# When accumulating loads may start, and weights split two units at a time

## The chip, the cores and the metric

The kernel runs on one core of a Trainium2 chip. The metric is the time of one execution on the device in microseconds (us). The core has a matrix engine (TensorE, PE in the profile), a vector engine (VectorE, DVE), an engine for activation functions (ScalarE, ACT), a general one (GpSimd, POOL) and one that mainly issues transfers (SyncE, SP). Transfers run on 16 DMA engines that all queues share.

## The reference

Three steps follow each other, all in fp32:

- Attention on q, k, v of shape (4 batches, 8 heads, 576 positions, 64). Every position attends to its neighbours at a distance under 4 (the local part). Beside it, q, k and v are averaged over groups of 4 positions, a full softmax attention runs over the 144 averaged positions, and its output is repeated 4 times and added (the down-sampled part).
- The 2304 token rows of 512 go through a gated layer: `silu(x @ w_gate) * (x @ w_val) @ w_out`, inner width 1536.
- Then through a second layer: `h = x @ w_in`, `h * clip(h + 3, 0, 6) / 6 @ w_out`, inner width 2048.

## The kernel before

**Blocks and units.** The token rows are worked in five blocks of 8, 6, 8, 8 and 6 groups of 64 rows, so that matmuls have 512 or 384 columns. Each block runs 68 units. A unit is one slab of 128 inner columns of a weight: G, V and O for the first layer (36 units, phase 1), H and P for the second (32 units, phase 2). One unit is about 12 matmuls, which `run_unit` issues (L951 for G, V, H; L993 for O, P).

**Weights.** Each fp32 number is split into a high and a low part, and three products are summed. The split of a unit's weights is `split_unit`: a ScalarE copy of 128x512 writes the high part (L234), a VectorE subtraction of 128x512 writes the low part (L235). They go into the tile `wr`, which has four buffers of one unit. In block 0 the weights arrive as 64-bit numbers of 512 KB a unit (`load_raw`, tile `w`, four buffers); `decode_a` on ScalarE (L214) and `decode_b` on VectorE (L223) make fp32 of them, in pairs of units in a staging tile of three buffers, and ScalarE's queue stores each pair to memory (`kept`, L229). Blocks 1 to 4 load these pairs back on SP's queue (`load_kept`, L182, 512 KB a pair) into the same staging buffers. `prefetch(i)`, called at every unit, says how many units ahead each step runs: raw load 8, kept load 6, decode 5 and 4, split 2 (`LS`).

**The down-sampled part.** For batches 1 to 3, `down_sums` fills three tiles dnq, dnk and dnv with sums over four positions: GpSimd's queue issues 24 transfers of 144 KB per batch (L295), the first of each tile plain and the next three accumulating into it, so that the four of one half of one tile follow each other. The order is position by position, and q, k, v within one. The work for batch b+1 is interleaved with block b: at every odd unit of phase 1 one step is issued, first the transfers, then TensorE's transposes of q and k (L306, from unit 25 on); in phase 2 `down_main` runs scores, softmax and values (L876 to L909). The last reader of dnv is the matmul pO (L726). GpSimd has nothing else to do then, so its queue runs ahead of the program until a buffer isn't free.

**The local part.** Chunks of q, k and v are loaded on SP's queue by `load_chunk` (L130), and VectorE works scores (L785, L788) in phase 1 and values (L822 to L828) in phase 2; `step_x` transposes the result (L842) and adds the down-sampled part (L851) for a block two further on.

**Batch 0** is done in `first_batch` ahead of block 0, with a pool of its own: its tile `fvd` holds the sums of v, `fpT` (two buffers) the transposed probabilities. The transfers of `down_sums(1)` are issued in it.

**Order.** Instructions are placed on each engine by a planner that works with estimated costs; `keep_in_program_order` marks those that it may not move ahead of what stands before them. Each engine, and each queue, then runs its list in that order. `put_out` at a block's end copies the outputs to the tile `os` on ScalarE (L1018) and stores them.

Of the kernel before, what the change touches and what calls it, by code (L numbers as in the profile page):

```python
# [10 lines left out]
F32 = mybir.dt.float32  # L11
F32R = mybir.dt.float32r
BF16 = mybir.dt.bfloat16
I32 = mybir.dt.int32
I16 = mybir.dt.int16
I64 = mybir.dt.int64
F16 = mybir.dt.float16
AF = mybir.ActivationFunctionType
ALU = mybir.AluOpType
AX = mybir.AxisListType  # L20

P = 128
# [5 lines left out]
BLOCKS = [8, 6, 8, 8, 6]  # L28

CUTS = [[3, 2], [2, 2, 2, 2], [3, 2, 3], [3, 3], []]  # L30
LR, LD, LA, LB, LS = 8, 6, 5, 4, 2
WARM = 14
HALVES = 1
CLOAD = (0, 4)
# [11 lines left out]
def tile_kernel(  # L46
# [12 lines left out]
    nc = tc.nc  # L59

    B, H, S, D = q.shape
    DM = H * D
# [4 lines left out]
    NJH = NJ // 2  # L67
    W = 7
    NC = DM // P
# [7 lines left out]
    UMAX = max(BLOCKS)  # L77
# [6 lines left out]
    sp = ctx.enter_context(tc.tile_pool(name="sp", bufs=2))  # L84
# [3 lines left out]
    def bank(tag, name, bufs=1):  # L88
        return pp.tile([P, 512], F32, tag=tag, name=name, bufs=bufs)
# [10 lines left out]
    consts = cp.tile([P, SMALL // 4], F32, name="consts")  # L100
# [27 lines left out]
    def late(eng, dst, src):  # L128

        tc.keep_in_program_order(eng.dma_start(dst, src))  # L130
# [3 lines left out]
    def behind(ins):  # L134

        if front[0]:
            tc.keep_in_program_order(ins)
# [5 lines left out]
    units = []  # L143
# [17 lines left out]
    w32 = {}  # L161
    split = {}

    def view(t, i):
        return t[:, i % 2, :].rearrange("p (c e) -> p c e", c=NC)
# [63 lines left out]
            defer(1, lambda: nc.scalar.dma_start(kept[i // 2], t))  # L229

    def split_unit(i):
        s = view(w32[i // 2], i)
        r = sp.tile([P, 2, NC, P], F32R, tag="wr", name=f"wr{i}", bufs=4)
        behind(nc.scalar.activation(r[:, 0], s, AF.Copy))  # L234
        behind(nc.vector.tensor_tensor(r[:, 1], s, r[:, 0].bitcast(F32), op=ALU.subtract))  # L235
        split[i] = r

    def prefetch(i):
        steps = ((LR, load_raw), (LD, load_kept), (LA, decode_a), (LB, decode_b), (LS, split_unit))
        for ahead, fn in steps:  # L240
            if 0 <= i + ahead < len(units):
                fn(i + ahead)


    tick_no = [0]
# [24 lines left out]
        nc.vector.tensor_tensor(dst[:, :, 1], xv, dst[:, :, 0].bitcast(F32), op=ALU.subtract)  # L270


    nat = {}
    dn, qk = {}, {}

    def load_down(b, what, half, hh, alloc, eng):
        src = {"q": q, "k": k, "v": v}[what]
        t = alloc(f"n{what}{b}_{half}{hh}")
        late(
            eng, t,  # L280
            src[b, hh * 4:hh * 4 + 4, half * NJH * 4:(half + 1) * NJH * 4, :].rearrange("h (j t) d -> j h t d", t=4),
        )
        nat[b, what, half, hh] = t

    keys = [(w, half, hh) for w in "qkv" for half in range(2) for hh in range(2)]

    def down_sums(b, dn, qk, alloc, bufs, eng, lag=0):
        for w in "qkv":
            dn[w] = sp.tile([NJH, 2, H, D], F32, tag="dn" + w, name=f"dn{w}{b}", bufs=1)
        for t in range(4):  # L290
            for w in "qkv":
                src = {"q": q, "k": k, "v": v}[w]
                for half in range(2):
                    s_ = src[b, :, half * NJH * 4:(half + 1) * NJH * 4, :].rearrange("h (j t) d -> j t h d", t=4)[:, t]
                    tc.keep_in_program_order(nc.gpsimd.dma_start(  # L295
                        dn[w][:, half], s_, **({"accum_op": ALU.add} if t else {})))
                yield

    def sums_T(b):
        for w in "qk":  # L300
# [20 lines left out]
    def first_batch():  # L321

        QT = 122
        WK = QT + 6
        NT = -(-S // QT)
        GT = 6
        TT = S // GT
        with tc.tile_pool(name="fp", bufs=1) as fp:
# [36 lines left out]
            nc.gpsimd.memset(band[:, :, 2, nl - 3:nl], NEG)  # L365


            vd = fp.tile([NJH, 2, H, D], F32, name="fvd")

            def load_vd(n):  # L370
                hh, half = divmod(n, 2)
# [40 lines left out]
            load_vw(4)  # L412
            assert NT == 5
            prefetch(2 - LR)

            tmp = spare("tmp")
# [110 lines left out]
            def size(i):  # L527
                return min(QT, S - QT * i)
# [49 lines left out]
                )  # L578

            pT = {}  # L580

            def trans(i):
                n = size(i)
                w_ = n + 6
                pT[i] = fp.tile([WK, NC, 2, QT], F32, tag="fpT", name=f"fpT{i}", bufs=2)
                for hh in range(2):
                    ps = bank(f"acc{2 + hh}", f"fPT{i}_{hh}")[:, :4 * QT]
                    ps = ps.rearrange("p (c a s) -> p c a s", c=2, a=2)
                    for m in range(4):
                        nc.tensor.transpose(  # L590
                            ps[:w_, m // 2, m % 2, :n], pe[i][:n, 2 * hh + m // 2, m % 2, :w_], ident[:n, :n]
                        )
                    to = pT[i][:w_, 2 * hh:2 * hh + 2, :, :n]
                    nc.scalar.activation(to, ps[:w_, :, :, :n], AF.Copy)
# [39 lines left out]
                    put_cols(bi, t0 + a - starts[bi] * UT, xf[:, :, a:e])  # L634
                    a = e

            turns = [0]

            def spare_tile(name):

                turns[0] += 1
                if turns[0] % 3 == 0:
                    return fp.tile([NJH, H // 2, 4, D], F32, tag="vnat", name=name, bufs=2)
                t = fp.tile([TT, GT, H // 2, D], F32, tag="fnat", name=name, bufs=4)
                t = t.rearrange("j t h d -> j (t h d)")[:NJH, :2 * H * D]
                return t.rearrange("j (h t d) -> j h t d", h=H // 2, t=4)


            ahead = down_sums(1, dn, qk, spare_tile, 6, nc.sync)
            for c in range(NC):  # L650
                load_T("q", c)
                load_T("k", c)
# [146 lines left out]
    def chunk_exp(b, c, n):  # L799
        sc, _ = pes[b, c]  # L800

        tc.keep_in_program_order(nc.scalar.activation(sc, sc, AF.Exp, scale=0.125))
# [129 lines left out]
    state = {}  # L932
# [98 lines left out]
    b, u = 1, 0  # L1031
    for n in chain(*CUTS):
# [3 lines left out]
        if u == NG:  # L1036
            b, u = b + 1, 0
# [4 lines left out]
    def load_ahead(n):  # L1042
        nonlocal loaded
        while loaded < min(n, len(chunks)):
            load_chunk(*chunks[loaded])
            loaded += 1

    NAT = 4

    def nat_tile(name):  # L1050
        t = sp.tile([P, 4 * DM + 32], I16, tag="w64", name=name, bufs=NAT).bitcast(F32)
        return t[:NJH, :2 * H * D].rearrange("j (h t d) -> j h t d", h=H // 2, t=4)

    for bi in range(NB):
        mine = chunks[at:at + len(CUTS[bi])]
        at += len(mine)
        limit = starts[bi + 2] if bi + 2 <= NB else 0

        db = bi + 1 if bi + 1 < B else None

        def first_half():
            for m, ch in enumerate(mine):
                for _ in chunk_scores(*ch):
                    yield
                load_ahead(at - len(mine) + m + 3 if m + 3 <= len(mine) else loaded)
            for _ in range(VAL0.get(bi, 0)):
                unit_values()
                yield

        def weigh(ch):  # L1070
            chunk_exp(*ch)
            vq.extend((*ch, i) for i in range(ch[2]))

        def second_half():
            for ch in mine[1:] if bi in VAL0 else mine:
                weigh(ch)
            while vq:
                unit_values()
                yield

        gens = [first_half(), second_half()]
        sizes = [sum(CUTS[bi]) + VAL0.get(bi, 0), sum(CUTS[bi]) - VAL0.get(bi, 0)]
        main = iter(())
        sums = iter(())
        if db:
            sums = down_T(db, dn, qk)
            if bi:
                sums = chain(down_sums(db, dn, qk, nat_tile, NAT, nc.sync, lag=1), sums)
        for i in range(bi * NU, (bi + 1) * NU):
            m = i - bi * NU  # L1090
            prefetch(i)
            if m in CLOAD:
                load_ahead(at - len(mine) + min(CLOAD.index(m) + 1, len(mine)))
            if m == EXP_AT and bi in VAL0:
                weigh(mine[0])
            run_unit(i)
            ph = 0 if m < NU1 else 1
            if m == NU1:
                for _ in gens[0]:
                    pass  # L1100
                for _ in sums:
                    pass
                if db:
                    main = down_main(db, dn, qk)
            lo_, n_ = (0, NU1 - 2) if ph == 0 else (NU1, NU - NU1 - 6)
            mm_ = m - lo_
            for _ in range(sizes[ph] * (mm_ + 1) // n_ - sizes[ph] * mm_ // n_ if mm_ < n_ else 0):
                next(gens[ph], None)
            if m % 2:
                next(sums, None)  # L1110
            next(main, None)
            if m == NU - EARLY:
                load_ahead(at + 1)
            step_x(limit)
            next_tick()
        if bi + 1 < NB:
            for _ in gens[1]:
                pass
            for _ in main:
                next_tick()  # L1120
            while x_done[0] < starts[bi + 2]:
                step_x(limit)
                next_tick()
# [30 lines left out]
```

## Time and profile before

| | |
|---|---|
| median of 3 runs | 981.95 us (980.12 to 983.34) |
| the profiled execution's own time | 982.72 us |
| its span, first to last instruction | 980.9 us |
| busy: TensorE / VectorE / ScalarE / GpSimd | 944.0 / 748.5 / 528.5 / 106.8 us |
| mean granted TensorE clock | 0.979 of full speed |
| transfers on GpSimd's queue | 43488 packets, 10.72 MB, 10.9% of the 16 DMA engines' span |

Busy time is an average over stages that differ. A TensorE that is shown as busy is not always at its peak, since matmuls are pipelined and their ends are modelled. What a change is worth is read where TensorE's list has a gap.

### The profile page before, as it was taken

The page shows a single profiled execution, that of the slowest core. Times are in us where ns is not written, and L with a number is a line of the kernel's source. Part 1 is how long each engine was busy: PE and PEld are TensorE (multiplying, and loading weights), DVE is VectorE, ACT ScalarE, POOL GpSimd, SP SyncE. Part 2 cuts the span into 40 slices and gives each one's busy share as a digit, 9 for nine tenths or more (in the row PEclk, how much of TensorE's full clock was granted, in tenths as well). Part 3 has the DMA queues.
Part 4 walks back from the last instruction along what each step waited for, and adds up shares of the span by engine and source line. Part 5 has one row for each costly group of instructions (what it writes and reads, how often), then busy time and mean ns, then how long its engine had stood idle before and what let it go on. Part 6 is the DMA issues. An engine that isn't in the chain of part 4 may idle for free.

```text
span 980.9 us, 13441 instructions
## 1 busy us (share of the span) xinstructions
PE 944.0 (96%) x4800; PEld 795.3 (81%) x4800; DVE 748.5 (76%) x1237; ACT 528.5 (54%) x1115; POOL 106.8 (11%) x113
## 2 busy tenths in 40 slices
PE   8878999999799999999999999999999999999997
PEld 5666878777699987888888777788888788999996
DVE  6578976898789988999684699999346995555653
ACT  4685566985554557655333764453335445544653
POOL 5941000007300000460000000000000000000000
PEclk9788999999899999999999999999999999999999
DMA  8999899469985432596432213353322223533331
GB/s 210 183 277 323 291 332 301 151 227 233 297 248 185 161 126 66 137 241 211 159 120 86 80 51 108 141 203 110 105 91 103 86 93 113 161 129 124 122 127 48
DMA packets 116343, 160.82 MB, mean 164 GB/s; under 512 B 61868, under 2 KB 83756, under 8 KB 116276
## 3 DMA queue, kind: packets, MB, share of 16 engines
q1 hardware_dynamic: 67892, 131.41, 40.9%
q0 software_dynamic: 43488, 10.72, 10.9%
q10 hardware_dynamic: 4896, 17.83, 4.8%
q8 instruction: 38, 0.62, 0.3%
q14 instruction: 29, 0.24, 0.1%
HBM read 137.29 MB, written 22.54 MB: 163 GB/s over the span
## 4 chain that ended last, share of the span: by engine, by line
PE 66%; DVE 12%; DMA 5%; issue 2%; ACT 2%; SPq 0%; ACTq 0%; DVEq 0%
PE pH L951 15%; PE aP L993 14%; PE aO L993 12%; PE pV L951 11%; PE pG L951 10%; DVE wr L235 3%; DVE pv L822 2%; DMA w<-in_moe_w_out_dram 1%; DMA k<-in_k_dram 1%; DVE xf L851 1%; DMA w<-in_moe_w_in_dram 1%; PE pS L876 1%; DVE pv L826 1%; DVE gH L969 1%; DVE h L967 1%
## 5 line engine op out<-in xcount | busy, mean ns | idle before, releaser
L235 DVE TENSOR_TENSOR wr<-w,wr 128x512 fp32r<-128x512 f32 x340 | 231.9, 686 | 115.8 <-ACT wr L234 114.2
L234 ACT ACTIVATE wr<-w 128x512 fp32r<-128x512 f32 x340 | 212.4, 627 | 163.8 <-PE pV L951 53.8
L951 PE MATMUL pH<-x,wr 128*128 128x512 f32 (+1 forms) x960 | 213.6, 374 | 0.0
L993 PE MATMUL aP<-wr,gH 128*128 128x512 f32 x864 | 211.0, 394 | 0.1
L951 PEld LDWEIGHTS pH<-x,wr 128*128 128x128 f32 x960 | 174.2, 189 | 26.2 <-issue 3.1
L993 PEld LDWEIGHTS aP<-wr,gH 128*128 128x128 f32 x864 | 159.6, 188 | 34.1 <-issue 2.1
L951 PE MATMUL pG<-xr,wr 128*128 128x512 f32 (+3 forms) x732 | 160.1, 374 | 7.7 <-ACT xr L269 4.0
L951 PEld LDWEIGHTS pG<-xr,wr 128*128 128x128 f32 x732 | 135.8, 194 | 26.3 <-ACT xr L269 4.4
L951 PE MATMUL pV<-xr,wr 128*128 128x512 f32 (+1 forms) x720 | 153.6, 368 | 1.2 <-ACT sl L957 1.2
L993 PE MATMUL aO<-gV,wr 128*128 128x512 f32 (+1 forms) x720 | 154.3, 370 | 0.2 <-DVE wr L235 0.2
L993 PEld LDWEIGHTS aO<-gV,wr 128*128 128x128 f32 x720 | 132.3, 190 | 17.4 <-DVE wr L235 0.5
L951 PEld LDWEIGHTS pV<-xr,wr 128*128 128x128 f32 x720 | 130.8, 188 | 18.6 <-ACT sl L957 1.9
L966 ACT ACTIVATE h<-pH,consts 128x512 f32<-128x512 f32 (+1 forms) x80 | 51.4, 642 | 67.9 <-PE pH L951 67.8
L214 ACT ACTIVATE top<-w 128x512 f16<-128x512 bf16 x68 | 53.7, 792 | 40.2 <-DMA w<-in_moe_w_in_dram 10.3
L967 DVE SCALAR_TENSOR_TENSOR h<-h,pH 128x512 f32<-128x512 f32 (+1 forms) x80 | 50.4, 631 | 25.4 <-ACT h L966 24.8
L957 ACT ACTIVATE sl<-pG 128x512 f32<-128x512 f32 (+1 forms) x60 | 33.2, 553 | 64.6 <-PE pG L951 62.9
L785 DVE TENSOR_TENSOR pr<-q,k 128x1792 f32<-128x1792 f32 x27 | 54.5, 2018 | 9.2 <-DMA k<-in_k_dram 9.2
L295 POOL DMA_DIRECT2D dnv<-in_v_dram x24 | 38.3, 2021 | 190.1 <-PE pO L726 181.9
L969 DVE TENSOR_TENSOR gH<-h,gH 128x512 fp32r<-128x512 f32 (+1 forms) x80 | 50.6, 633 | 9.2 <-ACT gH L968 8.3
L822 DVE TENSOR_TENSOR pv<-sc,v 128x1792 f32<-128x1792 f32 x27 | 54.6, 2021 | 0.4
L788 DVE TENSOR_REDUCE sc<-pr 128x28 f32<-128x1792 f32 x27 | 54.3, 2011 | 0.1
L968 ACT ACTIVATE gH<-h 128x512 fp32r<-128x512 f32 (+1 forms) x80 | 46.9, 587 | 13.9 <-DVE h L967 11.9
(124 smaller groups left out, 767.3 us busy)
## 6 DMA issues: line engine op xcount, KB each, us to landing
w<-kept SPq DMA_DIRECT2D x136, 512.0 KB
kept<-w ACTq DMA_DIRECT2D x34, 512.0 KB
w<-in_moe_w_out_dram SPq DMA_DIRECT2D x28, 512.0 KB
w<-in_moe_w_in_dram SPq DMA_DIRECT2D x16, 512.0 KB
w<-in_moe_w_gate_dram SPq DMA_DIRECT2D x12, 512.0 KB
w<-in_moe_w_val_dram SPq DMA_DIRECT2D x12, 512.0 KB
out_dram<-os SPq DMA_DIRECT2D x16, 256.0 KB
dnq<-in_q_dram POOLq DMA_DIRECT2D x24, 144.0 KB, 9.7
```

The costliest lines, as they stand in the source:

```text
L214: behind(nc.scalar.activation(halves(top[i % 2], 2, F16)[:, :, 1], h3.bitcast(BF16), AF.Copy))
L234: behind(nc.scalar.activation(r[:, 0], s, AF.Copy))
L235: behind(nc.vector.tensor_tensor(r[:, 1], s, r[:, 0].bitcast(F32), op=ALU.subtract))
L785: nc.vector.tensor_tensor(pr, qt[:, a:a + SUB, None, :].to_broadcast([P, SUB, W, D]), win(kt, a, SUB), op=ALU.mult)
L788: nc.vector.tensor_reduce(sc[:, a:a + SUB], pr, axis=AX.X, op=ALU.add)
L822: nc.vector.tensor_tensor(pr, pe[:, a:a + SUB, :, None].to_broadcast([P, SUB, W, D]), win(vt, a, SUB), op=ALU.mult)
L951: nc.tensor.matmul(ps[:, cs], r[:, a, c], x[:, c, b_, cs], start=part is HIGH and a == c == 0, stop=part is LOW and c == NC - 1,)
L966: nc.scalar.activation(h, ps, AF.Relu, scale=1 / 6, bias=half1[:, 0:1])
L967: nc.vector.scalar_tensor_tensor(h, h, 1.0, ps, op0=ALU.min, op1=ALU.mult)
L968: nc.scalar.activation(g[:, 0, :nt], h, AF.Copy)
L969: nc.vector.tensor_tensor(g[:, 1, :nt], h, g[:, 0, :nt].bitcast(F32), op=ALU.subtract)
L993: nc.tensor.matmul(ps, **one, start=f_ == 0 and a == b_ == 0, stop=f_ == nf - 1 and b_ == 1,)
```

## The change

- `down_sums` for batches 2 and 3 begins with a GpSimd copy of one column out of `os` of the preceding block, taken from its third piece of outputs (e = 2). So all its transfers wait until that block's outputs are written.
- The order of its transfers is q and k first, all four positions, then v. The tiles are allocated at their first transfer.
- `split_unit` does nothing for odd units, and for an even one splits the pair with one ScalarE copy and one VectorE subtraction of 128x1024. `wr` has three buffers of a pair in the place of four of one unit. `LS` is 3, so units i+3 and i+4 are split at odd i; the pair of units 2 and 3 is split at unit 0.
- To make room, `fvd` takes the buffer of dnv, and `fpT` becomes two halves of one `wr` buffer.
- Functions that nothing called are gone.

```
-LR, LD, LA, LB, LS = 8, 6, 5, 4, 2
+LR, LD, LA, LB, LS = 8, 6, 5, 4, 3
...
     def split_unit(i):
-        s = view(w32[i // 2], i)
-        r = sp.tile([P, 2, NC, P], F32R, tag="wr", name=f"wr{i}", bufs=4)
-        behind(nc.scalar.activation(r[:, 0], s, AF.Copy))
-        behind(nc.vector.tensor_tensor(r[:, 1], s, r[:, 0].bitcast(F32), op=ALU.subtract))
-        split[i] = r
+        if i % 2:
+            return
+        s = w32[i // 2].rearrange("p u (c e) -> p u c e", c=NC)
+        r = sp.tile([P, 2, 2, NC, P], F32R, tag="wr", name=f"wr{i}", bufs=3)
+        behind(nc.scalar.activation(r[:, :, 0], s, AF.Copy))
+        behind(nc.vector.tensor_tensor(r[:, :, 1], s, r[:, :, 0].bitcast(F32), op=ALU.subtract))
+        split[i], split[i + 1] = r[:, 0], r[:, 1]
...
-            if 0 <= i + ahead < len(units):
+            if 0 <= i + ahead < len(units) and (fn is not split_unit or i != -1):
                 fn(i + ahead)
+        if i == 0:
+            split_unit(2)
...
+    def down_sums(b, dn, qk):
+        if b > 1:
+            done = state["os"]
+            tc.keep_in_program_order(nc.gpsimd.tensor_copy(consts[:, 60:61], done[:, (UMAX // 2 - 2) * DM:][:, :1]))
+        for ws in ("qk", "v"):
+            for t in range(4):
+                for w in ws:
+                    if t == 0:
+                        dn[w] = sp.tile([NJH, 2, H, D], F32, tag="dn" + w, name=f"dn{w}{b}", bufs=1)
+                    src = {"q": q, "k": k, "v": v}[w]
+                    for half in range(2):
+                        tok = src[b, :, half * NJH * 4:(half + 1) * NJH * 4, :].rearrange("h (j t) d -> j t h d", t=4)
+                        how = {"accum_op": ALU.add} if t else {}
+                        tc.keep_in_program_order(nc.gpsimd.dma_start(dn[w][:, half], tok[:, t], **how))
+                    yield
...
-            vd = fp.tile([NJH, 2, H, D], F32, name="fvd")
+            vd = sp.tile([NJH, 2, H, D], F32, tag="dnv", name="fvd", bufs=1)
...
+            turned = sp.tile([P, 2, 2, NC, P], F32R, tag="wr", name="turned", bufs=3).bitcast(F32)
+            turned = turned.rearrange("p u a c e -> p u (a c e)")
...
-                pT[i] = fp.tile([WK, NC, 2, QT], F32, tag="fpT", name=f"fpT{i}", bufs=2)
+                pT[i] = turned[:WK, i % 2, :NC * 2 * QT].rearrange("p (c a s) -> p c a s", c=NC, a=2)
```

## Rows read from the trace of the kernel before

**Rows 1.** Stretches: length; busy (count) PE, PEld, DVE, ACT, POOL; clock; DMA; GB/s

```profile
224.00:268.00 44.00, 37.26 (x163) 29.75 (x160) 34.60 (x63) 24.38 (x42) 26.73 (x20) 0.92 1.21 266
...
281.00:312.00 31.00, 31.00 (x181) 30.92 (x179) 24.84 (x32) 14.75 (x27) 0.00 (x0) 1.00 0.61 214
312.00:341.00 29.00, 28.80 (x171) 28.50 (x170) 28.97 (x44) 15.37 (x30) 0.52 (x1) 1.00 0.50 172
...
543.00:646.00 103.00, 102.46 (x501) 79.31 (x500) 93.94 (x177) 60.13 (x142) 0.00 (x0) 1.00 0.29 97
```

**Rows 2.** TensorE's instructions in order of time: start, us, line, what

```profile
81.06 8.47 PE L951 MATMUL pG<-xr,wr 128*128 128x512 f32 x24 [3.45 <-DVE sl L963]
...
250.76 0.66 PE L842 MATMUL px<-ident,o 128*128 128x128 f32 x2 [6.34 <-DVE o L828]
251.07 7.16 PE L951 MATMUL pH<-x,wr 128*128 128x512 f32 x24
258.07 5.60 PE L993 MATMUL aP<-wr,gH 128*128 128x512 f32 x24
...
335.28 0.42 PE L306 MATMUL pqT<-ident,dnq 72*128 72x72 f32 x4
```

**Rows 3.** ScalarE's instructions in order of time

```profile
242.05 0.79 ACT L214 ACTIVATE top<-w 128x512 f16<-128x512 bf16 x1 [2.03 <-DMA w<-in_moe_w_out_dram]
247.78 0.78 ACT L214 ACTIVATE top<-w 128x512 f16<-128x512 bf16 x1 [4.94 <-DMA w<-in_moe_w_in_dram]
...
279.52 0.60 ACT L1018 ACTIVATE os<-aP 128x512 f32<-128x512 f32 x1 [0.76 <-PE aP L993]
...
453.45 0.63 ACT L234 ACTIVATE wr<-w 128x512 fp32r<-128x512 f32 x1 [2.50 <-DMA w<-kept]
```

**Rows 4.** The chain that ended last, in order of time: start, us, what

```profile
131.75 7.44 DMA w<-in_moe_w_out_dram
...
236.58 11.12 DMA w<-in_moe_w_in_dram
...
287.68 6.50 DMA k<-in_k_dram
...
302.81 6.38 DMA k<-in_k_dram
```

**Rows 5.** GpSimd's instructions in order of time

```profile
226.13 2.85 POOL L295 DMA_DIRECT2D dnq<-in_q_dram  x2
...
255.18 1.37 POOL L295 DMA_DIRECT2D dnq<-in_q_dram  x1 [5.52 <-DMA dnq<-in_q_dram]
...
407.74 2.85 POOL L295 DMA_DIRECT2D dnq<-in_q_dram  x2
...
423.83 3.57 POOL L295 DMA_DIRECT2D dnq<-in_q_dram  x2
```

**Rows 6.** The tile dnq: time of its transfers from issue to landing

```profile
DMA to landing us min/median/max: 3.3/9.7/21.3
```

**Rows 7.** Groups of instructions by line and shape: busy us, mean ns, idle before

```profile
L235 DVE TENSOR_TENSOR wr<-w,wr 128x512 fp32r<-128x512 f32 x340 | 231.9, 686 | 115.8 <-ACT wr L234 114.2
```

**Rows 8.** VectorE's instructions in order of time

```profile
47.60 1.22 DVE L575 TENSOR_TENSOR held<-held,fsm 122x1024 f32<-122x1024 f32 x1
48.74 0.66 DVE L270 TENSOR_TENSOR xr<-fxf,xr 128x488 fp32r<-128x488 f32 x1
...
74.43 2.02 DVE L785 TENSOR_TENSOR pr<-q,k 128x1792 f32<-128x1792 f32 x1 [4.25 <-DMA k<-in_k_dram]
...
222.69 0.68 DVE L223 SCALAR_TENSOR_TENSOR w<-w,top 128x512 int32<-128x512 int32 x1
...
232.94 0.69 DVE L223 SCALAR_TENSOR_TENSOR w<-w,top 128x512 int32<-128x512 int32 x1
...
348.13 1.28 DVE L235 TENSOR_TENSOR wr<-w,wr 128x512 fp32r<-128x512 f32 x2
```

**Rows 9.** SP's queue in order of time: when transfers were issued

```profile
283.93 3.22 SPq L182 DMA_DIRECT2D w<-kept  x2
```

More of the change, by code (lines that the diff above doesn't have):

```diff
@@ L270, in put_cols @@
         nc.vector.tensor_tensor(dst[:, :, 1], xv, dst[:, :, 0].bitcast(F32), op=ALU.subtract)
-    nat = {}
     dn, qk = {}, {}
[L276 to L297, printed above, removed]
+    def down_sums(b, dn, qk):
[13 more added lines that the diff above has]
+                    yield
     def sums_T(b):
@@ L635, in values @@
                     a = e
[L637 to L649, printed above, removed]
+            ahead = down_sums(1, dn, qk)
             for c in range(NC):
@@ L1046, in load_ahead @@
             loaded += 1
[L1048 to L1052, printed above, removed]
     for bi in range(NB):
@@ L1087, in tile_kernel @@
             if bi:
-                sums = chain(down_sums(db, dn, qk, nat_tile, NAT, nc.sync, lag=1), sums)
+                sums = chain(down_sums(db, dn, qk), sums)
         for i in range(bi * NU, (bi + 1) * NU):
```

## The prediction

> **What bounds the kernel now.** I read the stretches first, to see where TensorE's list has gaps; then TensorE's, ScalarE's and VectorE's instructions in order of time around each gap; then GpSimd's and SP's queues, to see what was in flight. TensorE is the bound of nearly the whole span, so work off TensorE is worth something only at its gaps. The largest gap within the blocks lies late in block 0: from 224 to 268 us TensorE is busy 37.26 of 44 us and the clock falls to 0.92 [rows 1]. The reader is to see one gap of 6.34 us there, and after it 24 matmuls that take 7.16 us where the next 24 take 5.60 [rows 2]. The gap ends when VectorE delivers a tile `o`, but behind that stands ScalarE, which waited 4.94 us for a raw weight load and 2.03 us for the one before [rows 3]. That load was issued at 236.58 and took 11.12 us, where another on the chain took 7.44 us [rows 4]. What was in flight beside it are the accumulating loads for batch 2, on GpSimd's queue at 226 to 256 us [rows 5], and the DMA share is 1.21 [rows 1]. Block 1 is a second weak place, of another kind: from 312 to 341 us VectorE is busy 28.97 of 29 us [rows 1]. Phase 2 of block 2 comes near that, with 93.94 of 103 us.
>
> **The change part by part.** Terms go against the profiled execution, 982.72 us.
>
> **(1) Batch 2's loads leave block 0.** They now wait for the third piece of block 0's outputs, which ScalarE writes at 279.52 to 280.12 [rows 3]. The raw load that took 11.12 us then has company like the one of 7.44 us, and lands 3.7 us earlier. The gap shrinks from 6.34 to 2.7 us, and of the 1.56 us that the low clock cost behind it (7.16 less 5.60) I give back the same share, 0.9 us. Taken: 4.6 us gained. Bounds: 7.9 us, when the gap and its clock loss vanish (6.34 + 1.56); nothing, when the gap has another cause (rival C).
>
> **(2) Where those loads go.** Block 1's head has a DMA share of 0.61 and then 0.50 [rows 1], so there is room, but on the chain stand two chunk loads of k, of 6.50 and 6.38 us [rows 4], for which VectorE's list waits in order. If the sums stretch them as they stretched the raw load (11.12 / 7.44 = 1.49), each is 3.2 us late, 6.4 us together. VectorE has 6.2 us idle in 281 to 312 us (31 less 24.84) and almost none after, so the first lateness is mostly covered and the second isn't. Against it: these loads stand on SP's queue behind kept loads, which waited 3.22 us from 283.93 for a staging buffer [rows 9]. The pair split frees that buffer at unit i-3 where it was i-1, so the k loads start earlier too, by up to those 3 us each. Taken: 2.0 us lost; bounds 0 and 6.4.
>
> **(3) Batch 3's loads leave block 1's end.** They were issued from 407.74 [rows 5]; now they start when block 1's outputs are done, and run beside block 2's head. There ScalarE waited for kept loads in front of its copies, 2.50 us in the longest case [rows 3], while the weights in hand kept TensorE going. Block 2's q and k are due only after 25 units of about 2.8 us (12 of the 24 matmuls in 5.60 us, rows 2), 70 us behind the gate. Taken: 1.0 us gained, bounds 0 and 2.5.
>
> **(4) Pairs.** 340 copies become 170, and 340 subtractions become 170. Back to back, a subtraction of 128x512 starts 0.60 us after the one before (two in 1.28 us, one alone 0.68), and behind an operation of 122x1024 the next starts after 1.14 us [rows 8]. A pair so saves 1.20 - 1.14 = 0.06 us of VectorE; where each stands alone, 2 x 0.686 - 1.22 = 0.15 us [rows 7, 8]. It counts where VectorE is nearly full: the 34 pairs of block 1 and 16 of block 2's phase 2. Taken 50 x 0.06 = 3.0 us gained; bounds nothing (hidden by TensorE) and 50 x 0.15 = 7.5 us. The other 120 pairs lie beside a busy TensorE and cost nothing; without that cover they would gain too. ScalarE's copies save alike, but ScalarE is at most 15.37 of 29 us busy there [rows 1]. What a pair costs is length: an evacuation behind a split waits for an operation of 1.2 us in the place of 0.69. TensorE has two buffers for its sums and 2 us per unit, which covers it. The third pair buffer gives three to four units of lead in the place of two; in return a pair's decode must be done for both units. I take 0 for both.
>
> The Trainium skill, in "VectorE: DVE Perf Modes", section "The TRN2 errata — SBUF-src ops pay a fixed extra latency per instruction", says that the cost of an instruction is exposed between instructions and one large tile pays it once; its fp32 formula, (N + 151) cycles at 0.96 GHz, would save 0.157 us a pair, by my estimate 7.9 us for the 50, and a median of about 970. The durations in rows 7 and 8 agree with that formula; the starts of back-to-back instructions don't, since they overlap by 0.08 us.
>
> **(5) The first batch.** q and k go first, v waits for the buffer of `fvd`. Its sums are needed only in block 0's phase 2. The bytes stay within a stretch where loads are late anyway: at 74.43 VectorE waits 4.25 us for k [rows 8], and TensorE 3.45 us, with 2.87 us of slow clock behind it (8.47 less 5.60, rows 2). v's eight loads move toward that moment, q's and k's away from it. Taken 0; bounds 6.3 us gained (that gap gone), 3.7 us lost (one load as late as in (1)). `fpT` as halves of one tile costs nothing, since TensorE's list puts the reader of a half ahead of its next writer.
>
> Sum: -4.6 + 2.0 - 1.0 - 3.0 + 0 = -6.6 us, 976.1 us against the profiled 982.72. The median lies 0.77 us below the profiled time, so 975.4 us.
>
> **The rivals.** A difference under 0.3% (2.9 us) can't be told from no change here.
>
> **A, the collision moves along.** Three chunk loads, not one, come late by 3.2 us, since VectorE is full from 312 us on: 9.6 us in place of 2.0. Time 983. For it speaks the DMA share of 1.21 beside the sums; against it the room and the earlier issue. The Trainium skill, in "DMA: Bandwidth & Descriptors", section "Queues, rings and completion order", says that an engine takes its queues in turn, packet by packet; by that rule sums slow whatever runs beside them, wherever they are put, which is this rival; the 11.12 us agree with it.
>
> **B, the sums come late (the other side).** The place is TensorE's first transpose of batch 2's q, unit 25 of block 1, at 335.28 us [rows 2]; behind it in TensorE's list stands all the rest. From the gate at 280.1 the q sums need three rounds and the last landing. A round was 8.0 us (407.74 to 423.83, two rounds) and 14.5 us (226.13 to 255.18, two rounds) [rows 5]; a landing took 9.7 us in the median, 21.3 at most [rows 6]. That gives 280.1 + 24 + 9.7 = 314 us, in time, or 280.1 + 43.5 + 21.3 = 345 us, 9.6 us late, and 1.6 us of slow clock as after the gap in block 0. Then -6.6 + 11.2 = +4.6: 986.6 us. It decides from rounds of 11.3 us with the longest landing ((335.3 - 280.1 - 21.3) / 3), 15.2 us with the median one. The slow rounds had v between q and k and raw loads beside them; the fast ones are nearer.
>
> **C, the relief doesn't show.** VectorE decoded no weights from 222.69 to 232.94 us [rows 8], because the planner put other work there, and a raw load needs the buffer that a decode frees. If that order makes the gap, it stays: (1) is 0, time 980.0.
>
> **D, more than that.** The gap goes altogether (7.9), pairs give 5 us, k loads lose nothing: 7.9 + 1.0 + 5.0 = 13.9, time 968.
>
> **How the numbers follow.** The forecast (971 to 979) has 0.48, D 0.12, C 0.16, A 0.10, B 0.14. Faster by over 0.3%, so under 979.0, are the forecast and D: 0.60. C and most of A are the same: 0.22. B and the rest of A are slower: 0.18. The range goes from 966, a little below D, to 987, B's price; 0.07 lies above it, with sums later than that, and 0.06 below.
>
> **What would show it.** (1) No GpSimd transfer from the first batch's to 280 us, no wait of ScalarE above 2 us for a raw load in 235 to 250 us, a gap there under 3 us. (2) k loads of 9 us at 285 to 310 us, issued earlier. (3) GpSimd silent from 406 to 440 us. (4) 170 operations of 1.2 us at L235's place, VectorE's sum about 25 us lower (170 x 0.15). B: a gap before pqT. Most likely to make it wrong: the planner orders a changed list anew, so that gaps arise or go that no row here shows.

## The result, and the profile after

The changed kernel takes 965.22 us (median of four executions, 964.39 to 967.08), 0.9832 [0.981, 0.9855] of the kernel before. Forecast were 975.4 us, so the gain was about 17 us where 6.6 were expected, and the time lies 0.8 us below the range. One of the four executions of the kernel before in that comparison took 1872.96 us and is left out. The same kernel beside the kernel before on two other chips gave 0.9894 [0.9871, 0.9918] (970.9 us) and 0.9853 [0.9818, 0.9887] (969.63 us): faster each time, by 10 to 17 us. These two medians lie inside the forecast range, so the miss of the range holds for the first comparison alone; that the gain was larger than forecast holds for all three. All 14 executions lie between 964.39 and 972.27 us.

To see where the time went, I cut each profiled execution on TensorE's list at the first matmul of a stage that stands behind the last one of the stage before (pH opens a block's phase 2, pG the next block). "Head" is everything ahead of block 0's phase 2. Each kernel has one such execution, and executions of one kernel differ by some us. Microseconds:

| kernel | head | block 0, phase 2 | block 1 (phase 1 + 2) | block 2 |
|---|---|---|---|---|
| before | 173.4 | 107.3 | 164.0 (81.1 + 82.9) | 200.8 |
| after | 166.9 | 103.1 | 158.9 (78.6 + 80.2) | 200.9 |

From block 3 on both take the same (335.5 and 335.6). The differences are -6.46, -4.26, -5.09 and +0.05, with +0.12 after them: -15.64 us, the difference of the spans (980.94 and 965.30). My terms for the same four stages were 0, -4.6, 0 (+2.0 for the loads, -2.0 for 34 pairs) and -2.0. So the surprise lies in the head and in block 1.

TensorE's instructions of the changed kernel in order of time (start, us, line, what, idle before):

```profile
79.04 5.74 PE L937 MATMUL pG<-xr,wr 128*128 128x512 f32 x24 [2.49 <-DVE sl L949]
...
255.28 0.66 PE L828 MATMUL px<-ident,o 128*128 128x128 f32 x2 [2.37 <-DVE o L814]
255.59 3.65 PE L937 MATMUL pH<-x,wr 128*128 128x512 f32 x9
259.08 11.05 PE L979 MATMUL aP<-wr,gH 128*128 128x512 f32 x48
...
324.07 0.41 PE L302 MATMUL pqT<-ident,dnq 72*128 72x72 f32 x4
...
345.20 0.41 PE L828 MATMUL px<-ident,o 128*128 128x128 f32 x2 [1.70 <-DVE o L814]
345.36 3.40 PE L979 MATMUL aO<-gV,wr 128*128 128x384 f32 x18
```

The gap of block 0 is still there, 2.37 us in the place of 6.34 [rows 2]. The 9 matmuls of pH behind it still run at a low granted clock, 0.51 of full speed at 255 to 257 us:

```profile
255.00:257.00 2.00, 1.72 (x5) 1.48 (x6) 1.12 (x5) 0.00 (x0) 0.00 (x0) 0.51 0.43 172
```

They take 3.49 us (255.59 to 259.08), where 9 of the 48 that follow at full clock (11.05 us) take 2.1. The first transpose of q, pqT, has no idle time before it.

GpSimd's instructions of the changed kernel, the gate and the rounds of batch 2's q:

```profile
93.17 1.37 POOL L292 DMA_DIRECT2D dnv<-in_v_dram  x1 [1.13 <-DMA dnv<-in_v_dram]
269.46 1.66 POOL L282 COPY consts<-os 128x1 f32<-128x1 f32 x1 [174.92 <-ACT os L1004]
...
276.76 2.81 POOL L292 DMA_DIRECT2D dnq<-in_q_dram  x2 [2.42 <-DMA dnq<-in_q_dram]
...
288.01 2.77 POOL L292 DMA_DIRECT2D dnq<-in_q_dram  x2 [5.64 <-DMA dnq<-in_q_dram]
...
298.83 2.81 POOL L292 DMA_DIRECT2D dnq<-in_q_dram  x2 [5.24 <-DMA dnq<-in_q_dram]
```

GpSimd is silent for 174.92 us until block 0's third output piece. A round then takes about 11 us, and the last one is issued 25 us before pqT.

The stretches that answer to [rows 1], in the changed kernel (length; busy and count of PE, PEld, DVE, ACT, POOL; clock; DMA; GB/s). Its stages begin 6 to 11 us earlier, so they hold slightly later work:

```profile
224.00:268.00 44.00, 41.33 (x179) 33.41 (x178) 39.66 (x65) 25.14 (x37) 0.00 (x0) 0.96 0.67 226
281.00:312.00 31.00, 31.00 (x181) 31.00 (x180) 29.15 (x29) 11.51 (x17) 14.17 (x11) 1.00 1.21 264
```

The DMA share of 1.21 has moved with the sums, from 224 to 268 us into 281 to 312 us, where TensorE is busy all the time.

### The profile page after: what moved, and what is told of

Same layout as the page of the kernel before. It is cut to its first block, busy times and chain, and to the rows that moved or that the text cites. A ratio compares the mean times of both kernels' runs of the same rounds, so it can differ in the third digit from the quotient of the medians.

```text
span 965.3 us, 12929 instructions
## 1 busy us (share of the span) xinstructions
PE 936.6 (97%) x4800; PEld 790.5 (82%) x4800; DVE 732.4 (76%) x1067; ACT 506.4 (52%) x945; POOL 109.2 (11%) x115
## 4 chain that ended last, share of the span: by engine, by line
PE 84%; DVE 9%; ACT 3%; issue 2%; DMA 1%; SPq 0%; ACTq 0%; DVEq 0%
PE pH L937 18%; PE aP L979 18%; PE aO L979 15%; PE pG L937 14%; PE pV L937 14%; DVE wr L237 2%; ACT held L560 1%; PE pS L862 1%; DVE pv L808 1%; DMA k<-in_k_dram 1%; PE pO L712 1%; DVE xf L837 1%; PE px L828 1%; PE pPT L705 1%; DVE h L953 1%
## 5 line engine op out<-in xcount | busy, mean ns | idle before, releaser
L237 DVE TENSOR_TENSOR wr<-w,wr 128x1024 fp32r<-128x1024 f32 x170 | 207.8, 1222 | 121.7 <-ACT wr L236 121.5
L236 ACT ACTIVATE wr<-w 128x1024 fp32r<-128x1024 f32 x170 | 179.7, 1057 | 128.8 <-issue 60.1
L937 PE MATMUL pG<-xr,wr 128*128 128x512 f32 (+3 forms) x732 | 155.0, 366 | 5.3 <-ACT xr L273 2.8
L937 PEld LDWEIGHTS pG<-xr,wr 128*128 128x128 f32 x732 | 132.2, 188 | 22.8 <-ACT xr L273 3.4
L954 ACT ACTIVATE gV<-sl 128x512 fp32r<-128x512 f32 (+1 forms) x60 | 35.0, 583 | 69.3 <-DVE sl L949 69.2
```

The lines of the kernel that those rows point to most:

```text
L236: behind(nc.scalar.activation(r[:, :, 0], s, AF.Copy))
L237: behind(nc.vector.tensor_tensor(r[:, :, 1], s, r[:, :, 0].bitcast(F32), op=ALU.subtract))
L937: nc.tensor.matmul(ps[:, cs], r[:, a, c], x[:, c, b_, cs], start=part is HIGH and a == c == 0, stop=part is LOW and c == NC - 1,)
L954: nc.scalar.activation(g[:, 0, :nt], h, AF.Copy)
```

## The experiments

The stage table for all runs, from one profiled execution each; the ratio is to the kernel before on the same chip:

| kernel | ratio | head | block 0, phase 2 | block 1 | block 2 |
|---|---|---|---|---|---|
| pairs_only | 0.9946 [0.9924, 0.9967] | 172.4 | 106.4 | 157.9 (77.2 + 80.6) | 200.3 |
| sums_only | 0.9978 [0.9963, 0.9994] | 171.2 | 99.6 | 164.6 (82.0 + 82.7) | 204.3 |
| no_gate | 0.9956 [0.9937, 0.9975] | 175.4 | 106.5 | 157.8 (77.2 + 80.6) | 200.3 |
| single_ops | 0.9939 [0.9915, 0.9963] | 173.6 | 101.1 | 162.4 (80.4 + 82.0) | 201.6 |
| head_only | 0.9934 [0.9914, 0.9954] | 168.3 | 107.4 | 160.1 (77.2 + 82.9) | 200.2 |
| old_order | 0.9948 [0.9933, 0.9962] | 173.6 | 103.2 | 162.4 (82.1 + 80.3) | 200.9 |
| after_again | 0.9894 [0.9871, 0.9918] | 169.7 | 104.1 | 158.1 (77.8 + 80.3) | 200.9 |
| after_third | 0.9853 [0.9818, 0.9887] | 169.7 | 103.3 | 158.1 (77.8 + 80.3) | 200.9 |
| gate_b2 | 0.9837 [0.9804, 0.9871] | 168.0 | 101.6 | 160.6 (79.7 + 80.9) | 200.2 |
| quiet | 0.9876 [0.9854, 0.9898] | 165.0 | 101.5 | 157.5 (77.2 + 80.3) | 200.8 |
| quiet_again | 0.9842 [0.9811, 0.9873] | 167.9 | 103.3 | 157.6 (77.3 + 80.3) | 200.9 |

**pairs_only**: the pairs and their buffers, without gate and with the old order of loads.

```diff
-        if b > 1:
-            done = state["os"]
-            tc.keep_in_program_order(nc.gpsimd.tensor_copy(consts[:, 60:61], ...))
-        for ws in ("qk", "v"):
+        for ws in ("qkv",):
-            vd = sp.tile([NJH, 2, H, D], F32, tag="dnv", name="fvd", bufs=1)
+            vd = fp.tile([NJH, 2, H, D], F32, name="fvd")
```

> Splits by pairs with three pair buffers and the lead of 3, and the halves of one buffer for the transposed probabilities, but the accumulating loads as before: no gate, q, k and v position by position, fvd in its own tile. Theory S (the loads' new place makes most of the 16 us): 978 to 980 us, the 3 us that the prediction gave to pairs, and the gap of 6 us at 244 us stays. Theory P (the pairs make most of it): 966 to 972 us, and the gap at 244 us shrinks too, since the plan of the decodes has changed.

976.48 us, 5.2 less than before; neither theory's range holds it. The gap of block 0 is 4.77 us long. Block 1 alone gives 6.1 (164.0 to 157.9), where I had taken 2.0. TensorE's rows show the place in its phase 1: first those of the kernel before at the end of block 1's phase 1, and VectorE's ahead of them.

```profile
356.73 0.66 PE L842 MATMUL px<-ident,o 128*128 128x128 f32 x2 [2.19 <-DVE o L828]
357.04 4.89 PE L993 MATMUL aO<-gV,wr 128*128 128x384 f32 x19
```

```profile
353.36 0.68 DVE L235 TENSOR_TENSOR wr<-w,wr 128x512 fp32r<-128x512 f32 x1
353.96 0.95 DVE L826 TENSOR_TENSOR pv<-pv 128x768 f32<-128x768 f32 x1
354.83 0.68 DVE L235 TENSOR_TENSOR wr<-w,wr 128x512 fp32r<-128x512 f32 x1
355.43 0.68 DVE L827 TENSOR_TENSOR pv<-pv 128x512 f32<-128x512 f32 x1
356.15 0.43 DVE L828 TENSOR_TENSOR o<-pv 128x256 f32<-128x256 f32 x1
```

The same places in pairs_only:

```profile
352.66 0.41 PE L825 MATMUL px<-ident,o 128*128 128x128 f32 x2 [0.37 <-DVE o L811]
352.83 3.39 PE L976 MATMUL aO<-gV,wr 128*128 128x384 f32 x18
```

```profile
350.38 0.95 DVE L809 TENSOR_TENSOR pv<-pv 128x768 f32<-128x768 f32 x1
351.37 0.69 DVE L810 TENSOR_TENSOR pv<-pv 128x512 f32<-128x512 f32 x1
352.09 0.42 DVE L811 TENSOR_TENSOR o<-pv 128x256 f32<-128x256 f32 x1
352.43 1.22 DVE L237 TENSOR_TENSOR wr<-w,wr 128x1024 fp32r<-128x1024 f32 x1
```

Before, a split stood right ahead of the sums that make `o` and another among them, TensorE waited 2.19 us for `o`, and the 19 matmuls behind it ran at first at a low granted clock (0.257 us each in the mean). With pairs the next split stands behind `o`: the gap is 0.37 us and a matmul takes 0.188 us. That is 1.8 us of gap and 1.3 us of clock, 3.1 of the 3.9 us of phase 1. The gap was in the trace of before, and my sum didn't have it. Where phase 2's 2.3 us went wasn't followed.

**sums_only**: the kernel before with the changed sums (gate, order, `fvd` in v's buffer) and single splits.

```diff
+        if b > 1:
+            done = state["os"]
+            tc.keep_in_program_order(nc.gpsimd.tensor_copy(consts[:, 60:61], ...))
+        for ws in ("qk", "v"):
...
-            vd = fp.tile([NJH, 2, H, D], F32, name="fvd")
+            vd = sp.tile([NJH, 2, H, D], F32, tag="dnv", name="fvd", bufs=1)
```

> The accumulating loads as in the changed kernel (gate on the preceding block's outputs, q and k first, v behind fvd), but splits by single units with four buffers and the lead of 2. Theory S: 968 to 972 us, with the gaps at 77 to 81 and 244 to 251 us gone. Theory P: 975 to 980 us, the gap at 244 us shorter and little else.

978.89 us, 2.8 less than before, in theory P's range. Block 0's phase 2 gives 7.7 us, almost the whole upper bound of 7.9 of step (1): the largest gap left there is 0.54 us.

```profile
242.85 0.41 PE L834 MATMUL px<-ident,o 128*128 128x128 f32 x2 [0.54 <-DVE o L820]
```

Block 1 costs 0.7 us and block 2 costs 3.5, and in both the loads beside the moved sums come late. In block 1 VectorE waits for a chunk of k and TensorE then for VectorE; in block 2's head ScalarE waits for a kept load, issued at 437.20 just behind the gate's copy and 9.60 us long, and TensorE for what hangs on it:

```profile
301.80 2.03 DVE L777 TENSOR_TENSOR pr<-q,k 128x1792 f32<-128x1792 f32 x1 [3.49 <-DMA k<-in_k_dram]
304.94 1.31 PE L985 MATMUL aO<-gV,wr 128*128 128x384 f32 x6 [2.56 <-DVE wr L235]
446.90 0.63 ACT L234 ACTIVATE wr<-w 128x512 fp32r<-128x512 f32 x1 [5.15 <-DMA w<-kept]
451.54 1.86 PE L943 MATMUL pG<-xr,wr 128*128 128x512 f32 x7 [2.78 <-DVE sl L955]
```

Neither gap is in the changed kernel. In its block 0, on the other hand, 3.5 of the 7.7 us are lost again (99.6 to 103.1): a gap behind `o` comes back. VectorE's rows of the changed kernel there show what stands ahead of `o`:

```profile
252.97 0.69 DVE L223 SCALAR_TENSOR_TENSOR w<-w,top 128x512 int32<-128x512 int32 x1 [2.10 <-ACT h L952]
253.58 1.22 DVE L237 TENSOR_TENSOR wr<-w,wr 128x1024 fp32r<-128x1024 f32 x1
254.72 0.42 DVE L814 TENSOR_TENSOR o<-pv 128x256 f32<-128x256 f32 x1
```

In single_ops, with the same buffers and lead but single operations, no gap in this phase behind `o` is left that reaches 0.3 us.

**no_gate**: the changed kernel without the three lines of the gate.

```diff
-        if b > 1:
-            done = state["os"]
-            tc.keep_in_program_order(nc.gpsimd.tensor_copy(consts[:, 60:61], ...))
```

> The changed kernel without the copy that makes the loads of batches 2 and 3 wait; q and k still go first. Theory S: the loads are back in block 0's phase 2 and at block 1's end, and 4 to 8 us are lost: 969 to 973 us. Theory P: 964 to 967 us, as the changed kernel.

976.68 us, above both ranges. The gate was worth more than pairs_only had let me think, and most of it in the head: 175.4 us, 8.5 above the changed kernel. GpSimd's rows of no_gate, the first and the last of the 12 rows that load batch 2's q and k in block 0's phase 1; TensorE's gaps there; and the stretch from 96 to 126 us:

```profile
93.25 2.25 POOL L289 DMA_DIRECT2D dnq<-in_q_dram  x2
...
142.51 1.37 POOL L289 DMA_DIRECT2D dnk<-in_k_dram  x1 [3.69 <-DMA dnk<-in_k_dram]
```

```profile
118.41 1.88 PE L934 MATMUL pV<-xr,wr 128*128 128x512 f32 x7 [1.47 <-ACT sl L940]
...
137.33 4.35 PE L934 MATMUL pV<-xr,wr 128*128 128x512 f32 x12 [2.30 <-ACT sl L940]
143.74 1.66 PE L934 MATMUL pV<-xr,wr 128*128 128x512 f32 x6 [2.06 <-ACT sl L940]
...
158.96 2.35 PE L934 MATMUL pV<-xr,wr 128*128 128x512 f32 x9 [1.33 <-ACT sl L940]
```

```profile
96.00:126.00 30.00, 28.54 (x126) 23.32 (x125) 22.14 (x26) 15.23 (x21) 12.21 (x10) 1.00 1.21 295
```

With q and k first and no gate, batch 2's loads begin as soon as batch 1's are done, beside block 0's raw loads: a DMA share of 1.21 where the changed kernel has 1.00, and 7.2 us of gaps. From 96 us to the head's end ScalarE, for which TensorE waits there, waits 28.9 us in all for raw loads; in the changed kernel it waits about 9 us. In the old order v comes third in the first round, and its buffer was in use. GpSimd's row of the kernel before shows that wait:

```profile
224.52 1.62 POOL L295 DMA_DIRECT2D dnv<-in_v_dram  x2 [127.05 <-PE pO L726]
```

GpSimd stood there for 127.05 us, until block 0's attention had read the old v, and the accumulating loads began at 226.13 [rows 5]. The old order held the loads back, and the new one needs the gate for that.

**single_ops**: the changed kernel, its pairs computed unit by unit (three pair buffers and the lead as in the change).

```diff
-        behind(nc.scalar.activation(r[:, :, 0], s, AF.Copy))
-        behind(nc.vector.tensor_tensor(r[:, :, 1], s, r[:, :, 0].bitcast(F32), op=ALU.subtract))
+        for u in range(2):
+            behind(nc.scalar.activation(r[:, u, 0], s[:, u], AF.Copy))
+            behind(nc.vector.tensor_tensor(r[:, u, 1], s[:, u], r[:, u, 0].bitcast(F32), op=ALU.subtract))
```

> The changed kernel with the pair buffers, the lead and the gate, but each pair split by two copies and two subtractions of 128x512 in the place of one of 128x1024. If the fixed cost per operation is what pairs give: 3 to 8 us lost, 968 to 973 us. If the lead and the buffers are what they give: 964 to 967 us.

975.61 us, above both ranges. Put between sums_only and the changed kernel, which share gate and order, it splits block 1's 5.8 us: buffers and lead 2.3 (164.6 to 162.4), wider operations 3.5 (162.4 to 158.9), or 4.3 against the repeats' 158.1, 0.10 to 0.13 us for each of 34 pairs. The two gaps of sums_only are gone, although VectorE still waits 3.42 us for k at 287.29 and ScalarE 4.6 us for a kept load in block 2's head: here buffers and lead cover the late loads. Its head of 173.6 has ScalarE waiting 5.38 us for a raw load at 96.49; why the same loads come late when the operations are single stays open.

**head_only**: pairs, no gate, the new order for batch 1 alone.

```diff
-        if b > 1:
...
-        for ws in ("qk", "v"):
+        for ws in ("qk", "v") if b == 1 else ("qkv",):
```

> Pairs, and the new order (q and k first, v behind fvd) for batch 1 alone; batches 2 and 3 as before, position by position and without a gate. Theory H (the gap at 80 us is closed by two parts together: the pairs let SP issue the first chunk load of k 2 us earlier, the late v lets it land 2 to 3 us sooner, and with the gap under 3 us the clock isn't lowered): against pairs alone 4 to 5 us are won in front of 96 us, 971 to 973 us, and the gap at 79 us is 2 to 2.7 us with full clock behind it. Rival (the pairs' head is as good alone, the changed kernel's head is the gate's doing): as pairs alone, 975 to 978 us, a gap of 3.5 us or more and slow clock.

973.99 us, between the two ranges; the head is 168.3 where pairs_only has 172.4, and block 0's phase 2 stays at 107.4. So in these two executions the order of batch 1 is worth 4 us in the head, once batch 2 stays away. The total doesn't show it (0.9934 and 0.9946, with intervals that overlap): block 1 takes 2.3 us more. The gap of the head was 2.68 us, and its 24 matmuls took 7.39 us, not the full clock that theory H had.

**old_order**: gate and pairs, q, k and v in turn as before.

```diff
-        for ws in ("qk", "v"):
+        for ws in ("qkv",):
-            vd = sp.tile([NJH, 2, H, D], F32, tag="dnv", name="fvd", bufs=1)
+            vd = fp.tile([NJH, 2, H, D], F32, name="fvd")
```

> The changed kernel with its gate, but q, k and v position by position in all batches, and fvd in its own tile. Theory H: the first chunk load of k has v's sums beside it again, the gap at 80 us is 3.5 us with a low clock behind it, and 4 to 5 us are lost there; the rest stays: 969 to 971 us. Rival (the gate alone counts): 964 to 967 us.

975.33 us, above both ranges. The gate gives its 3.2 us in block 0 (106.4 to 103.2) and more than that is lost in block 1's phase 1 (77.2 to 82.1): 3.1 us of gaps, where pairs_only has 0.4, and a low clock behind the last of them. The gap of the head is the longest of all. TensorE's rows of old_order:

```profile
83.59 7.90 PE L937 MATMUL pG<-xr,wr 128*128 128x512 f32 x24 [6.35 <-DVE sl L949]
...
336.31 0.47 PE L302 MATMUL pqT<-ident,dnq 72*128 72x72 f32 x4 [0.70 <-ACT qdT L313]
...
353.97 0.41 PE L828 MATMUL px<-ident,o 128*128 128x128 f32 x2 [1.70 <-DVE o L814]
354.14 4.93 PE L979 MATMUL aO<-gV,wr 128*128 128x384 f32 x18
```

With pairs, then: neither gate nor order 0.9946, order alone 0.9956, gate alone 0.9948, both 0.9832 to 0.9894. Each alone adds nothing that can be measured; together they take 5 to 11 us more.

**after_again, after_third**: the changed kernel, unchanged, beside the other runs.

> The changed kernel once more, beside the others of this group on the same chip: 964 to 967 us if its time is the kernel's own, some us more if part of the gain of 16 us was luck of one day.

> The changed kernel a third time, on the chip of the next two. Where it lies between 965 and 971 us is the question: theory H says that what differs between its executions is the head of block 0 alone (gap at 79 us of 2.5 us with full clock, or of 3 us with a low clock behind it, some 4 us apart), and that its blocks 1 to 4 take the same time within 1 us.

970.9 and 969.63 us; the first lies above the 964 to 967 us expected. From block 0's phase 2 on their stages are within about 1 us of the first execution's; the head is 2.8 us longer in both. TensorE's row and the stretch from 60 to 70 us of after_third, and then the same stretch of the first execution of the changed kernel:

```profile
80.22 7.36 PE L937 MATMUL pG<-xr,wr 128*128 128x512 f32 x24 [2.14 <-DVE sl L949]
```

```profile
60.00:70.00 10.00, 9.27 (x77) 8.31 (x78) 8.90 (x17) 8.90 (x21) 2.81 (x2) 0.81 0.93 228
```

```profile
60.00:70.00 10.00, 8.49 (x77) 7.19 (x77) 8.02 (x14) 8.90 (x16) 2.81 (x2) 0.98 0.99 276
```

A shorter gap, 2.14 against 2.49 us, is followed here by 24 matmuls that are partly at the low clock (7.36 against 5.74 us); the granted clock was already 0.81 at 60 to 70 us, against 0.98.

**gate_b2**: the gate for batch 2 alone.

```diff
-        if b > 1:
+        if b == 2:
```

> The changed kernel with the gate for batch 2 alone; batch 3's loads may start in block 1, q and k as soon as their tiles are free. The prediction's term for batch 3 was 1 us: then 1 us slower than the changed kernel, within 1 us in any case if block 1 isn't bound by transfers. If batch 3's loads hurt block 1 as batch 2's hurt block 0's head without a gate: 5 us slower.

967.84 us, beside 969.63 for the changed kernel on the same chip, with intervals that overlap: the gate of batch 3 isn't worth anything that the total shows. In the two blocks that it touches, gate_b2 takes 360.8 us (160.6 + 200.2) and the three executions of the changed kernel 358.9 to 359.7. The gate costs 0.6 us in block 2 and gives more than that in block 1, 1.1 to 1.9 us in all. What hides it is block 0, where in gate_b2 a gap of 2.38 us has no low clock behind it (101.6 us for 103.1 to 104.1).

**quiet**: batch 2's q and k are loaded at the start of block 0's phase 2 (gated on a tile written there), v at block 0's outputs; batch 3 as in the change.

```diff
+                if bi == 0:
+                    early = down_sums(2, dn, qk)
+                    for _ in range(8):
+                        next(early)
...
-            if bi:
+            if bi == 1:
+                sums = chain(early, iter([None] * 8), sums)
+            elif bi:
```

> A version to beat the changed kernel: batch 2's q and k sums start at block 0's phase 2, when the first layer's output is in place (about 167 us), where the DMA share was 0.54 to 0.60 up to 224 us; v's sums stay behind block 0's outputs. If block 1's head pays for the moved loads (78.6 against 77.3 us for its phase 1), 1 us or a little more is won: 963 to 965 us. If those 50 us are less quiet than the share says, since raw loads run there too, the gap at 255 us grows: 966 to 970 us.

> Batch 2's q and k sums in block 0's phase 2, once more, against the changed kernel on the same chip: 1 to 4 us faster than that if the first reading holds; no difference if it was the head of block 0 in few executions.

967.65 and 967.28 us, 3.2 and 2.4 below the changed kernel on the same chips, with overlapping intervals both times; block 1 is 0.5 us shorter (157.5 against 158.1). The remaining effect of the sums in block 1 is therefore small, and whether this version is better isn't settled.

## Why the prediction was wrong

**(5), the first batch: this step failed.** I took 0 and measured -6.5 us in the first execution, just over the upper bound of 6.3, and -3.7 in both repeats, each against the one profiled execution of the kernel before; so nearly 3 us of the first figure were luck. The bytes stay in the same stretch, as I wrote, but not in the same ten microseconds. First the stretch from 60 to 70 us of pairs_only, and then the load of k's first chunk in the chain of waits (start, us), of pairs_only and of the changed kernel:

```profile
60.00:70.00 10.00, 8.11 (x69) 7.01 (x68) 8.08 (x14) 8.65 (x15) 4.17 (x3) 0.84 1.26 258
```

```profile
63.25 10.94 DMA k<-in_k_dram
```

```profile
63.19 7.86 DMA k<-in_k_dram
```

The load is issued at the same time and lands 3.1 us earlier when the DMA share beside it is 0.99 and not 1.26: the last two of v's rounds are issued behind it, at 79.42 to 93.17 us. The pairs do the other half: before, SP issued this load at 65.09. Neither half does it alone. Pairs alone issue it 1.8 us earlier, but VectorE gets k at 74.32, before at 74.43; the order alone, in sums_only, has it issued at 66.69, and VectorE gets k at 76.09. In time, the first pG of that place starts 2.0 us earlier (81.06 to 79.04), its 24 matmuls take 2.7 us less (8.47 to 5.74), and 1.7 come later, 1.24 of them a gap at 140.56 us of the kernel before that is gone in pairs_only and sums_only too, so that its cause wasn't separated. I had named both prices, the gap and the clock, and then let the edit cancel itself. The Trainium skill, in "DMA: Bandwidth & Descriptors", section "Queues, rings and completion order", has the engine serve its queues in turn; the landing of 10.94 us beside the sums and of 7.86 without most of them agree with it. That a gap below 3 us leaves the clock alone, as I had come to think, fell with after_third; the changed kernel's own gap of 2.37 us in block 0, with the low clock behind it, had already spoken against it.

**What no step had: the gate and the order are one edit.** I added their terms. The four kernels with pairs show that each alone adds nothing that can be measured and both together 5 to 11 us: the new order takes away the wait that held batch 2's loads back by accident, and only the gate holds them back afterwards. The pairs belong to it too: without them gate and order gave 2.8 us (sums_only), since the moved loads then hit block 1 and block 2's head.

**(4), pairs: the term was mis-sized.** Block 1 gave 6.1 us with pairs alone, above the 5.1 of its upper price; block 2 gave 0.5. The spacing that I had used was right. VectorE's rows of the changed kernel:

```profile
305.62 1.22 DVE L237 TENSOR_TENSOR wr<-w,wr 128x1024 fp32r<-128x1024 f32 x1
306.75 2.02 DVE L774 TENSOR_REDUCE sc<-pr 128x28 f32<-128x1792 f32 x1
...
309.81 2.03 DVE L771 TENSOR_TENSOR pr<-q,k 128x1792 f32<-128x1792 f32 x1 [0.95 <-DMA k<-in_k_dram]
```

The next operation starts 1.13 us after a pair. What was missing is the lead with its buffers, taken as 0 and measured as 2.3 us in block 1 with the gate in place, and that a VectorE instruction ahead of `o` is paid in TensorE's gap and again in the clock behind it. What the wider operations give, 0.10 to 0.13 us a pair, is more than occupancy explains (0.06); the 0.157 us estimated from the Trainium skill's "VectorE: DVE Perf Modes", section "The TRN2 errata — SBUF-src ops pay a fixed extra latency per instruction", is more than was measured. The durations agree with it: 170 operations of 1222 ns against 340 of 686. VectorE's busy sum fell by 16 us (748.5 to 732.4), not 25. And pairs had a price that I took as 0: 3.5 us in block 0's phase 2, given the gate.

**(1) was right in its sum, -4.3 for -4.6, but not by its own mechanism alone.** The load's relief came: ScalarE waits for no raw load in 235 to 250 us. The gap fell by 4.0 us (6.34 to 2.37), where I had taken 3.7. The clock gave back 0.1 us and not 0.9: the matmuls behind the shorter gap still lose 1.4 us (3.49 less 2.1), before 1.56. "The same share" of the clock's price was wrong. Gate and order by themselves take 7.7 us there (sums_only), the case in which the gap vanishes, and the pairs give 3.5 back. The gap that is left waits for `o`, which stands behind a decode and a wide split in VectorE's list. So an order of VectorE's list, rival C's kind of cause, was partly at work, and, since single_ops has no such gap, the wide operations brought it.

**(2) was right in size.** The gate costs 1.4 us in block 1's phase 1 (77.2 to 78.6), and 0.5 in the repeats (77.8), with k waited for by 0.95 us at most, as in the last of the rows above; I had taken 2.0. TensorE pays it in the gap of 1.70 us at 345.20 (0.92 in the repeats).

**(3)** was near the 1.0 taken: 1.1 to 1.9 us in blocks 1 and 2 together by gate_b2, one execution, though its total doesn't show it.

**The rivals.** A did not come in the changed kernel, where no wait for k in block 1 exceeds 0.95 us. It did in sums_only, with TensorE's gaps of 2.56 and 2.78 us, so it was the pairs' buffers and lead that kept it away, which A did not have. B did not: pqT starts at 324.07 without a gap, although a round took 11 us, close to the 11.3 from which the longest landing would have decided. D, 968 us, came nearest to the time, and its 5 us for the pairs were near block 1's 6.1; its other two parts were not, since the gap in block 0 stayed and the gate cost 1.4 us.

## What to carry to other kernels

Before a new order of loads is costed, ask what held the later loads back in the old one: here a third stream's busy buffer was the gate, and with pairs the order and the explicit gate were worth 5 to 11 us only together. Where transfers are moved within a stretch, look at the ten microseconds around the load that the bound engine waits for, not at the bytes of the stretch. List every gap of the bound engine within the stages that a change touches: an instruction saved ahead of one was paid back twice, in the gap and in the clock behind it.

## What the runs showed of the hardware that was not expected

The 14 executions of the changed kernel differ by up to 0.8%, and between the three profiled ones nearly all of it lies in the head: 166.9, 169.7 and 169.7 us, with the clock at 0.98, 0.94 and 0.81 in the stretch from 60 to 70 us, and 24 matmuls at 5.74, 7.38 and 7.36 us behind gaps of 2.49, 3.09 and 2.14 us. The length of the gap ahead doesn't order them: the shortest of the three has the low clock behind it. Two more rows say the same. The gap at `o` in block 0 is 2.37 us in the changed kernel and 2.38 in gate_b2; the 9 matmuls behind it take 3.65 us there and 2.32 here. In quiet_again a gap of 2.92 us in the head has full clock behind it (a row of gate_b2, then one of quiet_again):

```profile
256.55 2.32 PE L937 MATMUL pH<-x,wr 128*128 128x512 f32 x9
79.99 5.76 PE L943 MATMUL pG<-xr,wr 128*128 128x512 f32 x24 [2.92 <-DVE sl L955]
```

So a gap of 2 to 3 us is a risk of 1.4 to 1.7 us more, by these rows, and not a fixed price. What decides there stays open.
